# First batch of an attention block: softmax weights divided while they are turned, x formed from PSUM

## The chip, the cores and the metric

The kernel runs on one core of one Trainium2 chip. The metric is the device time of one execution in microseconds (us). TensorE (PE in the rows, PEld its weight loads), VectorE (DVE), ScalarE (ACT), GpSimd (POOL) and the queue that issues the DMAs (SP) each run their own instructions in their own order and wait for one another by semaphores.

## The reference

Attention with a decay and a causal mask over 4 batches of 8 heads (576 positions, head size 64), then a gated feed-forward net, then a soft mixture of 8 expert nets. For the change only this part matters:

```python
attn = np.exp(scores)
attn = attn / (np.sum(attn, axis=-1, keepdims=True) + 1e-09)
return np.matmul(attn, v).astype(np.float32)
...
x = np.ascontiguousarray(attn_out.transpose(0, 2, 1, 3)).reshape(B * S, H * D)
x = _moe_ref(x=x, **moe_kwargs)
```

The softmax has a row sum for each of the 576 queries of a head. The division can be made before the product with v, after it, or anywhere between.

## The kernel before

**Stages.** `merge` lays streams of steps beside each other: first `attn_unit(0)` (attention of batch 0) with three calls of `convert` (weights of the first net, read from DRAM as 1 MB pieces, turned into floats and split into two parts); then attention of batch 1 with the first net on batch 0; and so on; last the expert nets. The order in each engine's queue is then set by a scheduler that plans all instructions by its own timing, across steps. So the first heads of batch 1 and the first products of the net on batch 0 (`pm`) already stand among the last heads of batch 0.

**One head of batch 0.** `load` fetches q and k (`qk`) and the decay row (`cb`), ScalarE and GpSimd split them. `scores(h, qi)` forms one of five query tiles in PSUM (`ps_s`), a custom VectorE instruction adds the decay and takes the minimum (`np`, `mn`), ScalarE takes the exponential and leaves the row sums in a column of `sm`. `trans(h, qi)` turns each 128x128 block of `np` on TensorE into PSUM (`ps_t`), with `nc.tensor.transpose` and the identity; VectorE (tiles 2 and 4, `ONV`) or ScalarE copies the group to `pt`. Per head that is 1+2+3+4 = 10 blocks of 128x128 and 5 blocks of 64x64 (the last tile has 64 queries, on partitions 64 to 127). `pv` multiplies the turned weights with v (`vs`) into `ps_o` in two ranges of queries, 256 and 320 wide; all operands are plain float32 in batch 0. ScalarE copies the result, not yet divided, to `bt`.

**After each pair of heads** `fold` divides. `recips` takes the ten columns of sums of the pair through ScalarE (adds 1e-9) and VectorE (reciprocal), turns them on TensorE (`ps_r`), copies them (`rt`), writes them to DRAM (`rd`) and reads them back, spread over 64 partitions each, with four DMAs (`rb`). GpSimd multiplies `bt` by `rb`, ScalarE rounds the product to `xh`, and GpSimd takes the remainder `xl`. `xh` and `xl` are what the first net reads; it sums over the four pairs of heads.

Of the kernel before, what the change touches and what calls it, by code (L numbers as in the profile page):

```python
# [8 lines left out]
F32 = mybir.dt.float32  # L9
# [24 lines left out]
def attention_two_ffns(ctx: ExitStack, tc: tile.TileContext, qkT, vt, f, wf, g2, w1, w2, out):  # L34
    nc = tc.nc
    B, H, D, _, S = qkT.shape
# [4 lines left out]
    P = 128  # L41
# [21 lines left out]
    ident = const.tile([P, P], F32, name="ident")  # L63
# [18 lines left out]
    xs = {}  # L82
# [57 lines left out]
    def rest(out, src, hi, eng=None):  # L140

        (eng or nc.gpsimd).tensor_tensor(out=out, in0=src, in1=hi.bitcast(F32), op=ALU.subtract)  # L142
# [42 lines left out]
    for i in range(2):  # L185
        nc.vector.memset(sms[i], 1.0)

    pts, vss = {}, {}

    def spaces(b):  # L190
# [13 lines left out]
    def attn_unit(b):  # L204
# [3 lines left out]
        def load_pair(hp):  # L208
            if hp == 0:
                xs[b] = [(xin0, xin1)[b % 2].tile([P, KD, S], F32R, tag=t, name=t) for t in ("xh", "xl")]  # L210
                if b < 2:
                    spaces(b)
            vs = vss[hp % 2]
            vr = vs if first else vp.tile([P, 5, P], F32, tag="vr", name="vr")
            src = vt[b, :, hp * P:(hp + 1) * P]
            nc.sync.dma_start(out=vr[:, 0:4, :], in_=src[0:512].rearrange("(j p) d -> p j d", p=P))
            nc.sync.dma_start(out=vr[64:128, 4, :], in_=src[512:576])
            if not first:
                v4 = vr.rearrange("p j (h d) -> p j h d", h=2)
                nc.scalar.copy(out=vs[:, 0:4, :, 0, :], in_=v4[:, 0:4])  # L220
                for h in range(2):
                    rest(vs[:, 0:4, h, 1, :], v4[:, 0:4, h], vs[:, 0:4, h, 0, :])
                nc.scalar.copy(out=vs[64:128, 4, :, 0, :], in_=v4[64:128, 4])
                rest(vs[64:128, 4, :, 1, :], v4[64:128, 4], vs[64:128, 4, :, 0, :])
            pairs[hp] = vs, btp.tile([P, S], F32, tag="bt", name="bt", bufs=2)

        def load(h):
            qk = raw.tile([P, 2, S], F32, tag="qk", name="qk")
# [25 lines left out]
                load_pair(h // 2)  # L254

        def scores(h, qi):
            a, kh, kl, cb, mn, nps = heads[h]
            sm, col = sms[h // 2 % 2], (h % 2 * 4 + qi if qi < 4 else 8 + h % 2)
            last = qi == 4
            qs, r0 = (448, 64) if last else (qi * P, 0)  # L260
            L = min((qi + 1) * P, S)
            pt = npp.tile([P, L], F32, tag=f"np{qi}", name="np")
            nps[qi] = pt
            chunks = ((0, 288, 288), (288, 288, 288)) if last else ((0, max(L, 256), L),)
            prev = 3.0e38
            for n, (c0, w, use) in enumerate(chunks):
                ps = (ps_m if first else ps_s).tile([P, 512], F32, tag="m" if first else "s", name="ps_s")
                nc.tensor.matmul(out=ps[:, 0:w], lhsT=a[:, qs:qs + P], rhs=kh[:, c0:c0 + w], start=True, stop=False)  # L268
                if c0 + use == L:
                    m0 = qs - c0  # L270
                    nc.tensor.matmul(out=ps[:, m0:m0 + P], lhsT=identb, rhs=maskb, start=False, stop=False)
                nc.tensor.matmul(out=ps[:, 0:w], lhsT=a[:, qs:qs + P], rhs=kl[:, c0:c0 + w], start=False, stop=True)  # L272
                m = mn[r0:P, qi + n:qi + n + 1]
                nc.vector.tensor_tensor_reduce(  # L274
                    out=pt[r0:P, c0:c0 + use], in0=ps[r0:P, 0:use], in1=cb[r0:P, c0:c0 + use], scale=-SCALE,
                    scalar=prev, op0=ALU.add, op1=ALU.min, accum_out=m)
                prev = m
            nc.scalar.activation(
                out=pt[r0:P, 0:L], in_=pt[r0:P, 0:L], func=AF.Exp, scale=-1.0, bias=prev,
                accum_out=sm[r0:P, col:col + 1])  # L280
# [18 lines left out]
            return rb  # L299

        def trans(h, qi):
            pt = heads[h][-1].pop(qi)
            alt = first and qi % 3 == 2
            ps = (ps_s if alt else ps_t).tile([P, 512], F32, tag="s" if alt else "t", name="ps_t")
            n, w, r0 = (qi + 1, P, 0) if qi < 4 else (5, 64, 64)
            pv = ps[:, 0:n * w].rearrange("p (j q) -> p j q", j=n)
            for j in range(n):
                k0 = min(j * P, 448)
                nc.tensor.transpose(pv[:, j, :], pt[r0:P, k0:k0 + P], ident[r0:P, r0:P])  # L309
            c = qi * P if qi < 2 else (qi - 2) * P  # L310
            if first:
                copy = nc.vector.tensor_copy if qi in ONV else nc.scalar.copy
                copy(out=pts[qi // 2 > 0][h % 2][:, 0:n, c:c + w], in_=pv)
                return
            hi, lo = pts[qi // 2 > 0]

            nc.scalar.copy(out=hi[:, 0:n, c:c + w], in_=pv)
            nc.vector.tensor_tensor(
                out=lo[:, 0:n, c:c + w], in0=pv, in1=hi[:, 0:n, c:c + w].bitcast(F32), op=ALU.subtract)

        def pv(h, rng):
            vs, bt = pairs[h // 2]
            e = h % 2
            w, t0 = ((WA, 0), (WB, 256))[rng]
            po = ps_o.tile([P, 512], F32, tag="o", name="ps_o")
            order = [0, 1] if rng == 0 else [0, 3, 4, 1, 2]
            rows, other = slice(64 * e, 64 * e + 64), slice(64 - 64 * e, 128 - 64 * e)
            b_ap = bt[rows, t0:t0 + w]
            if first:
                for i, j in enumerate(order):  # L330
                    c0, r0 = max(0, j * P - t0), (64 if j == 4 else 0)
                    nc.tensor.matmul(
                        out=po[:, c0:w], lhsT=vs[r0:P, j, :], rhs=pts[rng][e][r0:P, j, c0:w],
                        start=(i == 0), stop=(i == len(order) - 1))
                nc.scalar.copy(out=b_ap, in_=po[rows, 0:w])
                return
            ops = [(j, part) for j in order for part in range(2)]
            for i, (j, part) in enumerate(ops):
                c0 = 64 if rng and j >= 3 else 0
                nc.tensor.matmul(  # L340
                    out=po[:, c0:w], lhsT=vs[:, j, e].rearrange("p a d -> p (a d)"), rhs=pts[rng][part][:, j, c0:w],
                    start=(i == 0), stop=(i == len(ops) - 1))
            nc.scalar.copy(out=b_ap, in_=po[other, 0:w])
            nc.vector.tensor_tensor(out=b_ap, in0=po[rows, 0:w], in1=b_ap, op=ALU.add)
# [26 lines left out]
        for h in range(H):  # L371
            steps += [(c, lambda fn=fn, h=h: fn(h)) for c, fn in
                      ((0.3, load), (1.5, head_a), (2.0, front_b), (2.0, back_b))]
            if h % 2 == 1:
                steps.append((0.3, lambda hp=h // 2: fold(hp)))
        return steps

# [377 lines left out]
```

## Time and profile before

| what | us |
|---|---|
| median of 3 runs | 2269.47 |
| lowest and highest | 2268.91, 2271.68 |
| span of the profiled execution (first to last instruction) | 2267.1 |
| TensorE busy in it | 2224.7 (98%) |
| VectorE, ScalarE, GpSimd busy | 1689.3, 852.1, 887.4 |

The profiled execution's own time is known by its span alone; the median of the runs lies 2.4 us above that span, which is what lies around the first and the last instruction. How to read it: TensorE's 98% is a share of the whole, made up of stages. In the first slices of the page the busy shares of TensorE are 7 to 9 tenths, and VectorE, ScalarE, GpSimd and the DMA engines are all at 5 to 9 tenths there; after about 300 us TensorE stands at 9 in all slices. Batch 0's attention, the only part that the change touches, lies between about 10 and 110 us.

### The profile page before, as it was taken

The numbers are of one execution on the slowest core, as the hardware profiler recorded it, in microseconds if no ns is written. First come the engines' busy times: TensorE is split into PE (matmuls) and PEld (weight loads), VectorE is DVE, ScalarE is ACT, GpSimd is POOL, SyncE is SP. The second block draws the span as 40 slices with busy tenths as digits, with TensorE's granted clock in tenths as the row PEclk, the third lists the DMA queues.
The fourth block names the chain that finished last, engine by engine and source line by source line (L and its number), as shares of the span: only waits on it lengthen the run. The fifth ranks groups of instructions, "written<-read, shape, count | busy, mean of one in ns | idle before, by whom it ended". The sixth has DMA issues, their size and how long they took to land.

```text
span 2267.1 us, 36323 instructions
## 1 busy us (share of the span) xinstructions
PE 2224.7 (98%) x13881; PEld 2020.8 (89%) x13881; DVE 1689.3 (75%) x3385; ACT 852.1 (38%) x1952; POOL 887.4 (39%) x684
## 2 busy tenths in 40 slices
PE   7898999999999999999999999999999999999999
PEld 5698899999999888898988989889989899898897
DVE  6778854544535799887888878877788787887876
ACT  7866754454322434332322323223232232322321
POOL 6869863342423444332323323333233232332320
PEclk9999999999999999999999999999999999999999
DMA  9766664454644232111111111161111111111101
GB/s 249 204 204 217 217 228 159 164 170 146 236 161 154 89 119 94 59 56 38 47 47 38 56 38 47 49 224 56 38 47 47 38 56 38 47 47 38 56 29 52
DMA packets 105102, 232.50 MB, mean 103 GB/s; under 512 B 10672, under 2 KB 60128, under 8 KB 92896
## 3 DMA queue, kind: packets, MB, share of 16 engines
q1 hardware_dynamic: 104928, 230.18, 31.5%
q8 instruction: 109, 1.79, 0.3%
q14 instruction: 65, 0.53, 0.1%
HBM read 193.27 MB, written 36.87 MB: 102 GB/s over the span
## 4 chain that ended last, share of the span: by engine, by line
PE 85%; DMA 6%; DVE 5%; POOL 1%; ACT 1%; issue 1%; SPq 1%; POOLq 0%; DVEq 0%; ACTq 0%
PE py L150 39%; PE pa L601 30%; PE pm L150 10%; DMA st<-wf 3%; PE ps_o L340 1%; PE ps_t L309 1%; PE ps_s L272 1%; DMA xst<-xd 1%; PE ps_s L268 1%; DMA rb<-rd 1%; DVE al L616 1%; DVE np L274 0%; DMA rd<-rt 0%; DVE y L111 0%; DMA lgd<-ls 0%
## 5 line engine op out<-in xcount | busy, mean ns | idle before, releaser
L601 PE MATMUL pa<-xf,w1h 128*128 128x288 f32 x3584 | 748.8, 295 | 0.2 <-DVE u L610 0.2
L601 PEld LDWEIGHTS pa<-xf,w1h 128*128 128x128 f32 x3584 | 597.7, 188 | 37.8 <-DVE u L610 0.7
L653 DVE SCALAR_TENSOR_TENSOR acc<-py,lg,acc 128x512 f32<-128x512 f32 x531 | 395.2, 744 | 247.5 <-PE py L150 247.3
L601 PE MATMUL pa<-xf,w1l 128*128 128x288 f32 x1792 | 527.6, 295 | 0.0
L142 POOL TENSOR_TENSOR w2l<-w,w2h 128x1024 fp32r<-128x1024 f32 x64 | 154.6, 2416 | 820.5 <-ACT w2h L577 820.5
L150 PE MATMUL py<-w2h,ah 128*128 128x512 f32 x1152 | 454.2, 394 | 3.3 <-DVE acc L646 2.8
L150 PE MATMUL py<-w2l,ah 128*128 128x512 f32 x1152 | 454.1, 394 | 0.0
L150 PE MATMUL py<-w2h,al 128*128 128x512 f32 x1152 | 453.2, 393 | 0.0
L616 DVE SCALAR_TENSOR_TENSOR al<-c,ah 128x288 fp32r<-128x288 f32 x512 | 431.5, 870 | 5.4 <-ACT ah L615 4.7
L615 ACT ACTIVATE ah<-c 128x288 fp32r<-128x288 f32 x512 | 208.0, 443 | 566.4 <-PE py L150 319.5
L601 PEld LDWEIGHTS pa<-xf,w1l 128*128 128x128 f32 x1792 | 337.0, 188 | 10.6
L150 PE MATMUL pm<-xh,w 128*128 128x288 f32 x1536 | 326.3, 298 | 3.3 <-DVE xa L431 1.6
L150 PEld LDWEIGHTS py<-w2h,al 128*128 128x128 f32 x1152 | 216.3, 188 | 50.0
L150 PEld LDWEIGHTS pm<-xh,w 128*128 128x128 f32 x1536 | 252.0, 188 | 6.2 <-DVE xa L431 2.1
L150 PEld LDWEIGHTS py<-w2h,ah 128*128 128x128 f32 x1152 | 216.3, 188 | 32.6 <-DVE acc L646 3.2
L150 PEld LDWEIGHTS py<-w2l,ah 128*128 128x128 f32 x1152 | 216.3, 188 | 26.1
L150 PE MATMUL pm<-xl,w 128*128 128x288 f32 x768 | 226.2, 295 | 0.5 <-POOL xl L142 0.5
L621 ACT COPY m<-pa 128x288 f32<-128x288 f32 x128 | 50.3, 393 | 437.0 <-PE pa L601 434.8
L142 POOL TENSOR_TENSOR w1l<-w,w1h 128x256 fp32r<-128x256 f32 x192 | 162.3, 873 | 125.1 <-ACT w1h L573 125.1
L150 PE MATMUL py<-ah,w 128*128 128x288 f32 x768 | 174.6, 299 | 4.8 <-DVE th L413 2.5
L142 POOL TENSOR_TENSOR al<-th,ah 128x288 fp32r<-128x288 f32 x96 | 83.6, 871 | 203.0 <-ACT ah L415 200.7
L142 POOL TENSOR_TENSOR w1l<-sm,w1h 128x1024 fp32r<-128x1024 f32 x64 | 153.7, 2401 | 2.5 <-ACT w1h L573 2.5
(145 smaller groups left out, 3109.4 us busy)
## 6 DMA issues: line engine op xcount, KB each, us to landing
w<-w SPq DMA_DIRECT2D x128, 512.0 KB, 3.5
w<-wsplit SPq DMA_DIRECT2D x54, 1024.0 KB, 5.5
qk<-qkT SPq DMA_DIRECT2D x64, 288.0 KB, 6.2
st<-wf SPq DMA_DIRECT2D x18, 1024.0 KB, 8.7
wsplit<-w SPq DMA_DIRECT2D x18, 1024.0 KB, 4.7
cb<-cumd SPq DMA_DIRECT2D x31, 288.0 KB, 4.0
xo<-h SPq DMA_DIRECT2D x28, 288.0 KB, 2.2
xf<-xo SPq DMA_DIRECT2D x14, 576.0 KB, 10.1
```

The costliest lines, as they stand in the source:

```text
L142: (eng or nc.gpsimd).tensor_tensor(out=out, in0=src, in1=hi.bitcast(F32), op=ALU.subtract)
L150: nc.tensor.matmul(out=ps, lhsT=a, rhs=b, start=(i == 0), stop=(i == n - 1))
L268: nc.tensor.matmul(out=ps[:, 0:w], lhsT=a[:, qs:qs + P], rhs=kh[:, c0:c0 + w], start=True, stop=False)
L272: nc.tensor.matmul(out=ps[:, 0:w], lhsT=a[:, qs:qs + P], rhs=kl[:, c0:c0 + w], start=False, stop=True)
L309: nc.tensor.transpose(pv[:, j, :], pt[r0:P, k0:k0 + P], ident[r0:P, r0:P])
L340: nc.tensor.matmul(out=po[:, c0:w], lhsT=vs[:, j, e].rearrange("p a d -> p (a d)"), rhs=pts[rng][part][:, j, c0:w], start=(i == 0), stop=( ...
L601: nc.tensor.matmul(out=ps, lhsT=w[:, MW[m - 1], k], rhs=x[:, m - 1, hl, k], start=(n == 0), stop=(n == len(ops) - 1))
L615: nc.scalar.activation(out=ah[:, f, tk], in_=src, func=AF.Relu)
L616: nc.vector.scalar_tensor_tensor(out=al[:, f, tk], in0=src, scalar=0.0, in1=ah[:, f, tk].bitcast(F32), op0=ALU.max, op1=ALU.subtract)
L621: nc.scalar.copy(out=m1, in_=p1)
L653: nc.vector.scalar_tensor_tensor(out=a, in0=py, scalar=lg[:, t, e:e + 1], in1=a, op0=ALU.mult, op1=ALU.add)
```

## The change

For batch 0 only, the division moves ahead of the product with v. The row sums go to a tile of their own for each head (`sm0`, named `sn0` and `sn1`). At the first and third query tile of a head VectorE adds 1e-9 to two or three columns of sums and takes their reciprocals (`rq`). For each query tile VectorE then multiplies the identity by the column of reciprocals, which gives a diagonal matrix (`dg`, 128x128 or 64x64), and the turn becomes an ordinary matmul with `np` as the stationary operand and `dg` as the moving one, where `nc.tensor.transpose` had the identity. After `pv` ScalarE rounds PSUM straight to `xh` and VectorE takes the remainder straight from PSUM to `xl`. `fold` and `recips` are no longer called for batch 0; `bt` isn't allocated there. The other batches are as before.

```diff
+    sm0 = [small.tile([P, 5], F32, name=f"sn{i}") for i in range(2)]
+    for i in range(2):
+        nc.vector.memset(sm0[i], 1.0)
...
-            pairs[hp] = vs, btp.tile([P, S], F32, tag="bt", name="bt", bufs=2)
+            pairs[hp] = vs, None if first else btp.tile([P, S], F32, tag="bt", name="bt", bufs=2)
...
-            sm, col = sms[h // 2 % 2], (h % 2 * 4 + qi if qi < 4 else 8 + h % 2)
+            sm, col = (sm0[h % 2], qi) if first else (sms[h // 2 % 2], h % 2 * 4 + qi if qi < 4 else 8 + h % 2)
...
+            turn = ident[r0:P, r0:P]
+            if first:
+                if qi in (0, 2):
+                    g0, g1 = (0, 2) if qi == 0 else (2, 5)
+                    rc = small.tile([P, 5], F32, tag="rq", name="rq", bufs=2)
+                    nc.vector.tensor_scalar_add(out=rc[:, g0:g1], in0=sm0[h % 2][:, g0:g1], scalar1=1e-9)
+                    nc.vector.reciprocal(out=rc[:, g0:g1], in_=rc[:, g0:g1])
+                    heads[h] += (rc,)
+                rc = heads[h][-1]
+                dg = small.tile([P, P], F32, tag="dg", name="dg", bufs=3)
+                nc.vector.tensor_scalar_mul(out=dg[r0:P, 0:w], in0=turn, scalar1=rc[r0:P, qi:qi + 1])
+                turn = dg[r0:P, 0:w]
             for j in range(n):
                 k0 = min(j * P, 448)
-                nc.tensor.transpose(pv[:, j, :], pt[r0:P, k0:k0 + P], ident[r0:P, r0:P])
+                if first:
+                    nc.tensor.matmul(out=pv[:, j, :], lhsT=pt[r0:P, k0:k0 + P], rhs=turn, start=True, stop=True)
+                else:
+                    nc.tensor.transpose(pv[:, j, :], pt[r0:P, k0:k0 + P], turn)
...
-                nc.scalar.copy(out=b_ap, in_=po[rows, 0:w])
+                xh, xl = (t[rows, h // 2, t0:t0 + w] for t in xs[b])
+                nc.scalar.copy(out=xh, in_=po[rows, 0:w])
+                rest(xl, po[rows, 0:w], xh, nc.vector)
                 return
+            b_ap = bt[rows, t0:t0 + w]
...
-            if h % 2 == 1:
+            if h % 2 == 1 and not first:
                 steps.append((0.3, lambda hp=h // 2: fold(hp)))
```

The scheduler lays the queues out anew. On TensorE, where the first head of batch 0 is turned and multiplied, the kernel before has these rows in succession (`ps_s` is a score tile of the second head, `vs` is v):

```order
L309 MATMUL ps_t<-ident,np 128x128 x4
L309 MATMUL ps_t<-ident,np 128x64 x5
L272 MATMUL ps_s<-kl,qkh 128x256 x2
L272 MATMUL ps_s<-kl,qkh 128x384
L268 MATMUL ps_s<-qkh 128x512
L271 LDWEIGHTS identb
L271 MATMUL ps_s<-maskb,identb 128x128
L272 MATMUL ps_s<-kl,qkh 128x512
L332 MATMUL ps_o<-pt,vs 128x320
L332 MATMUL ps_o<-pt,vs 128x192
L332 MATMUL ps_o<-pt,vs 128x64
L332 MATMUL ps_o<-pt,vs 128x320 x2
```

On TensorE, in the changed kernel, from the first turn of the first head:

```order
L326 MATMUL ps_t<-dg,np 128x128 x3
L276 MATMUL ps_s<-kl,qkh 128x256 x2
L276 MATMUL ps_s<-kl,qkh 128x384
L326 MATMUL ps_t<-dg,np 128x128 x7
L272 MATMUL ps_s<-qkh 128x512
L275 LDWEIGHTS identb
L275 MATMUL ps_s<-maskb,identb 128x128
L276 MATMUL ps_s<-kl,qkh 128x512
L350 MATMUL ps_o<-pt,vs 128x256
L350 MATMUL ps_o<-pt,vs 128x128
L326 MATMUL ps_t<-dg,np 128x64 x5
L272 MATMUL ps_s<-qkh 128x288
```

The turns now read `dg`, and the first of them stands behind three score tiles of the second head; before, six turns and the first `ps_o` of the first head stood ahead of those.

On VectorE, in the kernel before, between the last score tiles of the first head and the first of the second (`ISA` is the custom instruction on a score tile, `y`, `g` and `st` belong to `convert`, `pt` is the copy of turned weights):

```order
L274 ISA np,mn<-ps_s,cb 64x288
L274 ISA mn 64x1
L116 TENSOR_SCALAR y<-g 128x1024
L274 ISA np,mn<-ps_s,cb,mn 64x288
L274 ISA mn 64x1
L117 SCALAR_TENSOR_TENSOR st<-st,y 128x1024
L313 COPY pt<-ps_t 128x3x128
L313 COPY pt<-ps_t 128x5x64
L274 ISA np,mn<-ps_s,cb 128x128
```

On VectorE, in the changed kernel, at the same place (`sn` holds the sums, `rq` the reciprocals):

```order
L316 TENSOR_SCALAR rq<-sn_197 128x2
L278 ISA np,mn<-ps_s,cb 64x288
L278 ISA mn 64x1
L116 TENSOR_SCALAR y<-g 128x1024
L317 RECIPROCAL rq<-rq 128x2
L278 ISA np,mn<-ps_s,cb,mn 64x288
L278 ISA mn 64x1
L117 SCALAR_TENSOR_TENSOR st<-st,y 128x1024
L321 TENSOR_SCALAR dg<-ident,rq 128x128 x2
L316 TENSOR_SCALAR rq<-sn_197 128x3
L317 RECIPROCAL rq<-rq 128x3
L321 TENSOR_SCALAR dg<-ident,rq 128x128 x2
```

Nine more instructions of this head (four on `rq`, five on `dg`, the fifth right behind the last row) stand ahead of the second head's score tiles, the first two `dg` stand behind a whole convert step on `st`, and the two copies `pt` have moved behind those score tiles.

On SP, in the kernel before, around the fold of the first pair of heads:

```order
L292 DMA rd_0_177<-rt 10x128
L231 DMA qk<-qkT 64x1152 x2
L243 DMA cb<-cumd 128x576
L297 DMA rb<-rd_0_177 64x512
L298 DMA rb<-rd_0_177 64x64
L297 DMA rb<-rd_0_177 64x512
L298 DMA rb<-rd_0_177 64x64
L126 DMA wsplit_113<-w 128x2048
L103 DMA st<-wf 128x4096
```

On SP, in the changed kernel, around the same second write of converted weights:

```order
L247 DMA cb<-cumd 128x576
L235 DMA qk<-qkT 64x1152
L221 DMA vs<-vt 64x128
L126 DMA wsplit_113<-w 128x2048
L220 DMA vs<-vt 128x4x128
L235 DMA qk<-qkT 64x1152
L103 DMA st<-wf 128x4096
```

The write `rd` and the four reads `rb` are gone from the queue, four times in all, and the weights' DMAs have moved up past loads of later heads.

## Rows read from the trace of the kernel before

**Rows 1.** Busy time by stretch, from:to in us; in brackets instructions
```profile
core 0: us, PE busy (x) PEld busy (x) DVE busy (x) ACT busy (x) POOL busy (x), PEclk, DMA share, GB/s
20.00:110.00 90.00, 78.59 (x450) 59.78 (x448) 70.51 (x180) 73.42 (x181) 73.35 (x54) 0.94 0.80 228
110.00:150.00 40.00, 40.00 (x294) 38.35 (x294) 27.10 (x60) 29.48 (x73) 29.36 (x25) 0.97 0.57 178
150.00:300.00 150.00, 139.78 (x987) 127.63 (x986) 124.26 (x274) 100.75 (x233) 126.89 (x100) 0.98 0.69 223
```

**Rows 2.** The same view, three stretches of 10 us inside batch 0
```profile
40.00:50.00 10.00, 7.17 (x34) 5.58 (x34) 7.31 (x17) 5.89 (x15) 5.90 (x4) 0.71 0.95 237
50.00:60.00 10.00, 9.47 (x60) 7.40 (x58) 8.95 (x26) 9.11 (x25) 7.88 (x6) 0.95 0.84 246
70.00:80.00 10.00, 9.52 (x55) 7.33 (x55) 5.90 (x19) 8.64 (x19) 9.29 (x8) 0.92 0.81 215
```

**Rows 3.** Chain that ended last, its TensorE pieces: start us, us, what
```profile
20.96 0.89 PE ps_t L309 x9
...
23.50 2.50 PE ps_o L332 x10
...
26.66 0.67 PE ps_t L309 x6
...
78.28 0.65 PE ps_o L332 x4
```

**Rows 4.** Timeline of weight loads: the two of one 64-row product of L332
```profile
24.30 0.29 PEld L332 LDWEIGHTS ps_o<-pt,vs 64*128 64x128 f32 x2 [0.23 <-issue]
```

**Rows 5.** VectorE by line and form, first 125 us: busy us, mean ns | idle before
```profile
L274 DVE CUSTOM_DVE_ANT_0 np<-ps_s,cb 128x128 f32<-128x128 f32 x12 | 3.5, 289 | 4.6 <-PE ps_s L272 4.1 <-DMA cb<-cumd 0.4
...
L286 DVE RECIPROCAL rc<-rc 128x10 f32<-128x10 f32 x5 | 1.1, 215 | 0.1
...
L344 DVE TENSOR_TENSOR bt<-ps_o,bt 64x256 f32<-64x256 f32 x2 | 0.8, 417 | 0.0
...
L344 DVE TENSOR_TENSOR bt<-ps_o,bt 64x320 f32<-64x320 f32 x1 | 0.5, 480 | 0.0
...
L66 DVE CAST identb<-ident 128x128 bf16<-128x128 f32 x1 | 0.2, 219 | 0.0
...
L79 DVE CAST gw<-gs 128x32 fp32r<-128x32 f32 x1 | 0.2, 184 | 0.8 <-DMA gs<-g 0.8
L72 DVE MEMSET ones<- 128x128 f32 x1 | 0.2, 165 | 0.8 <-PEq L748 0.8
...
L186 DVE MEMSET sm<- 128x10 f32 x2 | 0.1, 67 | 0.0
```

**Rows 6.** GpSimd and ScalarE by line and form, first 125 us: the fold
```profile
L142 POOL TENSOR_TENSOR xl<-bt,xh 128x576 fp32r<-128x576 f32 x4 | 6.3, 1578 | 0.0
...
L350 POOL TENSOR_TENSOR bt<-bt,rb 128x576 f32<-128x576 f32 x4 | 5.7, 1414 | 4.0 <-DMA rb<-rd 4.0
...
L351 ACT CAST xh<-bt 128x576 fp32r<-128x576 f32 x4 | 2.7, 672 | 0.0
```

**Rows 7.** Timeline, last pair: DMA write, last product on TensorE, last remainder
```profile
97.67 0.47 SPq L292 DMA_DIRECT2D rd<-rt  x1
...
98.94 2.66 PE L332 MATMUL ps_o<-pt,vs 128*128 128x320 f32 x10
...
110.26 1.42 POOL L142 TENSOR_TENSOR xl<-bt,xh 128x576 fp32r<-128x576 f32 x1
```

**Rows 8.** Timeline around 42 us, VectorE and TensorE: [idle before <- releaser]
```profile
41.76 1.00 DVE L111 TENSOR_SCALAR y<-st 128x1024 uint16<-128x1024 uint16 x1 [2.37 <-DMA st<-wf]
...
43.52 0.36 PE L268 MATMUL ps_s<-qkh 128*128 128x256 f32 x1 [2.83 <-DVE mn L274]
```

**Rows 9.** Waits of TensorE from 20 to 110 us: us, times, longest
```profile
PE ps_s L268 <- DVE mn L274: 6.3, 5, 2.8
PE ps_s L272 <- POOL kl L142: 1.8, 1, 1.8
```

More of the change, by code (lines that the diff above doesn't have):

```diff
@@ L256, in scores @@
         def scores(h, qi):
-            a, kh, kl, cb, mn, nps = heads[h]
-            sm, col = sms[h // 2 % 2], (h % 2 * 4 + qi if qi < 4 else 8 + h % 2)
+            a, kh, kl, cb, mn, nps = heads[h][:6]
+            sm, col = (sm0[h % 2], qi) if first else (sms[h // 2 % 2], h % 2 * 4 + qi if qi < 4 else 8 + h % 2)
             last = qi == 4
@@ L301, in trans @@
         def trans(h, qi):
-            pt = heads[h][-1].pop(qi)
+            pt = heads[h][5].pop(qi)
             alt = first and qi % 3 == 2
@@ L327, in pv @@
             rows, other = slice(64 * e, 64 * e + 64), slice(64 - 64 * e, 128 - 64 * e)
-            b_ap = bt[rows, t0:t0 + w]
             if first:
```

## The prediction

> **What bounds the kernel now.** I read the busy time by stretch first, since the 98% of the page hides the stage that the change touches. From 20 to 110 us, where batch 0's attention runs, TensorE is busy 78.6 of 90 us, VectorE 70.5, ScalarE 73.4, GpSimd 73.4, and the DMA engines 80% [rows 1]: five resources, each between 78% and 87%, none full. From 110 to 150 TensorE is busy without a gap, and from 150 to 300 it is busy 139.8 of 150 us. So a delay of the first stage is handed on: what comes after is TensorE's work in full, with some 10 us of idle up to 300 us that could take a little back. The question is how long the first stage becomes.
>
> In that stage TensorE has 11.4 us of idle (90 less 78.6). The largest part, 6.3 us, is waiting for VectorE to free a score buffer, and 1.8 us for GpSimd's split of k [rows 9]. One of those waits shows how it comes about: VectorE sat 2.37 us on a convert step whose weights had not landed, the score tiles stood behind it in its queue, and TensorE idled 2.83 us [rows 8]. Just after this the granted clock was 0.71 on average over 10 us [rows 2], that is, TensorE ran part of them at 1.2 GHz; over the stage it was 0.94 [rows 1]. The best that single stretches show is TensorE busy 9.52 of 10 us and VectorE 8.95 of 10 [rows 2]; I use these as the fullest the two get in this mixture of work.
>
> **TensorE: the turns become float32 products.** The chain of waits gives paces without the drain at the end. Six turns of 128x128 took 0.67 us, 0.112 each; nine turns, four of them 128x128 and five 64x64, took 0.89 us, which leaves (0.89 - 4 x 0.112) / 5 = 0.088 for a small one [rows 3]. The products of weights and v are float32 too and are ordinary matmuls, and each of their instructions appears as two passes: two instructions (256 and 128 columns) have x4 and took 0.65 us for 768 columns, 0.85 ns a column, so 0.108 us for a pass of 128 columns [rows 3]. A turn by a diagonal is such a product with 128 columns: two passes, 0.216 us, where a transpose takes 0.112. Batch 0 has 8 heads x 10 = 80 of them: 80 x 0.104 = +8.3 us.
>
> For the small turns (64 rows, 64 columns, 8 x 5 = 40) the row is the one product of the kind in each `pv`. Five products with ten passes took 2.50 us; eight passes with 2304 columns at 0.85 ns are 1.95, which leaves 0.55 for the two small passes, 0.27 each [rows 3], with the change of rows in and out in it. The other end is the pace of their weight loads: two took 0.29 us, with a single one at about 0.18, so they start 0.11 apart [rows 4]. Five turns in succession change rows once, so I take 0.13, near the load's end: per head 10 x 0.13 - 5 x 0.088 = 0.86, times 8 = +6.9 us (from 5.3 at 0.11 to 18.1 at 0.27). The four turns `ps_r` go, each a pass of 128 columns: 4 x 0.108 = -0.4 us. TensorE's sum is +14.8 us, with ends +13 and +26.
>
> The page "FP8 and Floating Point Precision" of the Trainium skill (section TensorE Precision Notes) gives true float32 four passes, and "TensorE: Matmul & The Clock Gate" (section Terms) calls its transpose mode four times faster for float32. The trace agrees with the first (two records at twice the time per column) but not with the second: a turn of 128 columns at 0.112 us is half a product's 0.216, not a quarter. By the pages the large turns would add 80 x 0.162 = 13 us where the rows give 8.3.
>
> **VectorE: diagonals, reciprocals, remainders.** None of these operations is in the trace of batch 0, so each has bounds [rows 5]. A diagonal of 128x128 (32 of them) lies between a memset of that size, 0.165, and the custom instruction on a 128x128 score tile, 0.289; I take 0.219, the copy of the same identity. 32 x 0.219 = 7.0. The eight small ones: 0.184, a 128x32 copy, 1.5 in sum (0.067 below). Sixteen additions on two or three columns: 0.184 by the same row, 2.9 (0.067 by a memset of ten columns). Sixteen reciprocals: 0.215 as the ten-column one, 3.4 (0.067 again below). Sixteen remainders `xl` from PSUM: eight at 0.417 and eight at 0.480, as the same form at L344, 7.2. Gone are four reciprocals and four copies `rt`, which I count like them: 8 x 0.215 = -1.7. The sum is +20 us, with ends +13 and +23.
>
> **The rest.** GpSimd loses four multiplications and four remainders, 5.7 + 6.3 = 12 us; ScalarE loses four roundings, 2.7 us [rows 6], and its 16 copies to `bt` become 16 roundings of the same size. SP loses 20 DMAs with their waits. I put these at nothing: neither engine is the one that TensorE mostly waits for, and at most the 1.8 us of rows 9 goes with them. If their cover were gone the other way there is nothing to pay, since they only lose work. The fold's latency also goes: the last pair's `rd` was issued at 97.67 and its last remainder ended at 110.26 + 1.42 = 111.7 us [rows 7]; with the change `x` is there about a copy and a remainder after the product. But TensorE has other work by then, and is busy throughout from 110 on, so that an earlier `x` finds no idle TensorE.
>
> **A new wait.** Each turn now waits for its diagonal, and this for reciprocals, and these for the last exponential of a group of two or three tiles. Queued behind the waiting diagonals on VectorE are the score tiles of the next head, the convert steps and the copies `pt`; TensorE waits for all of them. The new order answers by putting three score tiles of the second head ahead of the first turn, which holds more score buffers at a time.
>
> **The sum.** In the stage VectorE has 70.5 + 20 = 90.5 us to do in what were 90; at 0.895 busy that needs 101.1 us, +11.1. TensorE has 78.6 + 14.8 = 93.4; at 0.952 it needs 98.1 us, +8.1. The larger counts, since each waits for the other in turn: +11 us. Nothing later gives it back. On the profiled span, 2267.1 + 11 = 2278.1, and with the 2.4 us between span and median, **2280.5 us**. With both engines at the low ends (83.7 / 0.895 and 91.6 / 0.952) the stage grows by 4 to 6 us: 2275; with the high ends (93.5 / 0.895 and 104.6 / 0.952) by 14 to 20, of which I take 17, since 0.27 for every small pass counts the change of rows each time: 2287.
>
> **Rivals.**
> (1) *The new chain stalls the queues.* The idle that TensorE has stays on top of its sum: 93.4 + 11.4 = 104.8, +14.8; and in half of the eight heads the diagonals of the third group come late by one wait of the kind in rows 9 (6.3 / 5 = 1.26 us), +5. That gives +20, **2290 us**. For it: the 2.83 us of rows 8, where one VectorE instruction that waited held everything. Against it: the scheduler has put other work between.
> (2) *The clock makes up for part.* The granted clock over the stage is 0.94, and TensorE's low clock follows its pauses in the one case of rows 8 and 2. If fuller queues keep it at 2.4 GHz, TensorE's sum falls by 0.06 x 78.6 = 4.7 to 88.7, or 93.2 us at 0.952, +3; VectorE must then be near its low end (+3.5). That gives **2273 us**, within 0.2%. The Trainium skill, "TensorE: Matmul & The Clock Gate" (section Part 4: PE-mode transpose), speaks for it: transposes don't count as TensorE being busy in the way that matmuls do. By that rule the change turns 120 uncounted instructions into counted ones. The trace neither shows nor denies it: the fall in rows 2 has a plain pause before it.
> (3) *Faster: the fold was the pace.* If TensorE's 14.8 us fit into its 11.4 us of idle and the 4.7 us that the low clock costs, the stage stays at 90 us; then the 14 us from `rd` to the last remainder [rows 7] and GpSimd's 12 us [rows 6] let the first net run ahead, and half of the 10 us of idle from 150 to 300 [rows 1] closes: -5, **2264 us**. It decides as soon as VectorE has room for its 20 us; it has 19.5 us of idle in 90, and no stretch shows it full. That is what speaks against it.
> (4) *The change doesn't do what it says on TensorE*, that is, a product by a diagonal runs in one pass like a transpose. VectorE's sum stands, +11; this changes the reason and not the time, and has its chance inside the forecast.
>
> **How the numbers follow.** The forecast with its own range 2275 to 2287 gets 0.52, the stalled chain 0.16, the clock 0.18, the faster case 0.14. About 0.2% (4.5 us, so 2265 to 2274) is what a measurement of this kernel can tell from no change. Slower is the forecast and the stall, 0.68; same the clock, 0.18; faster 0.14. The range leaves out the faster case and the far side of the stall: 2265 to 2293.
>
> **What would show it.** Turns with two passes each and a pace near 0.22 us for 128 columns, near 0.26 for the small ones; diagonals near 0.22 us; VectorE busy some 90 us by the time the last `ps_o` of batch 0 ends, and this end some 11 us later than the 101.6 us of now [rows 7]; from there on the same distance to the end as before. The prediction is wrong if VectorE does its new work in its idle time and that end doesn't move, if the granted clock rises to 1.0 and TensorE's busy time in the stage stays below 90 us, or if the stretch from 150 to 300 closes its idle.

## The result, and the profile after

The changed kernel takes 2284.9 us (median of 5 runs, 2283.21 to 2287.61), the kernel before in the same comparison 2269.33 (5 runs, 2267.80 to 2271.68): a ratio of 1.007 with a 95% interval of 1.0057 to 1.0084, or +15.6 us. The forecast was 2280.5, slower. The profiled execution, 1.5 us above that median, has a span of 2284.6 us, against 2267.1.

Busy time of the engines of the changed kernel over the span, from its page:

```profile
PE 2241.1 (98%) x13997; PEld 2038.1 (89%) x13997; DVE 1711.1 (75%) x3467; ACT 850.1 (37%) x1944; POOL 870.2 (38%) x676
```

TensorE is busy 16.4 us longer than before and VectorE 21.8. Of the span, 17.5 us longer, TensorE was idle 2284.6 - 2241.1 = 43.5 us, where it was 42.4. So at the end TensorE's idle is what it was, and its added work is there in full. It is tempting to stop here and blame the second passes; the experiments say otherwise.

The same stretches as [rows 1, 2], now of the changed kernel:

```profile
core 0: us, PE busy (x) PEld busy (x) DVE busy (x) ACT busy (x) POOL busy (x), PEclk, DMA share, GB/s
20.00:110.00 90.00, 75.61 (x430) 60.63 (x429) 81.11 (x199) 54.93 (x127) 47.75 (x37) 0.92 0.64 194
110.00:150.00 40.00, 39.31 (x266) 33.92 (x265) 24.44 (x82) 29.54 (x76) 20.52 (x21) 1.00 0.42 120
150.00:300.00 150.00, 140.40 (x1008) 129.87 (x1006) 124.94 (x276) 104.97 (x246) 123.84 (x96) 0.98 0.67 220
40.00:50.00 10.00, 7.19 (x40) 5.57 (x40) 9.68 (x27) 7.48 (x17) 5.38 (x4) 0.76 0.37 93
50.00:60.00 10.00, 9.16 (x55) 7.54 (x54) 7.27 (x15) 3.13 (x6) 4.25 (x4) 0.90 0.75 247
70.00:80.00 10.00, 7.89 (x51) 6.39 (x51) 9.81 (x29) 6.45 (x18) 5.04 (x4) 1.00 0.72 263
```

From 20 to 110 us VectorE is now the fullest engine, 81.1 of 90 us where it had 70.5; in two of the short stretches it has no room left (9.68 and 9.81 of 10). ScalarE fell from 73.4 to 54.9 and GpSimd from 73.4 to 47.8: they have done less by then, in part because they have less to do. TensorE's idle rose from 11.4 to 14.4 us although it has more to do.

TensorE's waits from 20 to 125 us in the changed kernel (us, times, longest), to be set beside [rows 9]:

```profile
PE ps_t L326 <- DVE dg L321: 4.5, 6, 1.3
PE ps_s L272 <- DVE mn L278: 4.1, 7, 1.1
PE ps_t L326 <- DVE pt L332: 3.9, 2, 2.7
PE ps_o L350 <- DVE xl L142: 1.6, 1, 1.6
```

All of them end on VectorE, on four kinds of its work, and GpSimd's split of k is gone from the list. The new operations on VectorE up to 125 us (busy us, mean ns | idle before):

```profile
L321 DVE TENSOR_SCALAR dg<-ident,rq 128x128 f32<-128x128 f32 x32 | 20.3, 658 | 0.3
...
L316 DVE TENSOR_SCALAR rq<-sn 128x3 f32<-128x3 f32 x8 | 4.2, 521 | 0.9 <-ACT np L282 0.9
...
L321 DVE TENSOR_SCALAR dg<-ident,rq 64x64 f32<-64x64 f32 x8 | 3.9, 484 | 2.8 <-PE ps_t L326 2.6
...
L142 DVE TENSOR_TENSOR xl<-ps_o,xh 64x320 fp32r<-64x320 f32 x7 | 3.4, 484 | 0.2
...
L316 DVE TENSOR_SCALAR rq<-sn 128x2 f32<-128x2 f32 x8 | 2.0, 247 | 0.0
...
L317 DVE RECIPROCAL rq<-rq 128x3 f32<-128x3 f32 x8 | 1.4, 170 | 0.1
...
L317 DVE RECIPROCAL rq<-rq 128x2 f32<-128x2 f32 x8 | 1.3, 157 | 0.1
```

A diagonal of 128x128 takes 0.658 us on average, not 0.219, and all 40 take 24.2 us where the prediction had 8.5. The mean hides two kinds. Of the 40, 23 take 0.25 to 0.29 us, and 17 take 0.44 to 1.50. The timeline shows what parts them. First VectorE, then GpSimd, of the changed kernel near 57 us:

```profile
57.15 2.60 DVE L321 TENSOR_SCALAR dg<-ident,rq 128x128 f32<-128x128 f32 x2
```

```profile
57.16 1.41 POOL L142 TENSOR_TENSOR kl<-qk,qkh 128x576 fp32r<-128x576 f32 x1
58.52 2.26 POOL L122 TENSOR_TENSOR st<-st,g 128x512 f32<-128x512 f32 x2
```

And VectorE near 48.8 us, where GpSimd ran nothing from 47.5 to 50.5:

```profile
48.41 0.17 DVE L316 TENSOR_SCALAR rq<-sn 128x3 f32<-128x3 f32 x1
48.61 0.18 DVE L317 RECIPROCAL rq<-rq 128x3 f32<-128x3 f32 x1
48.83 0.48 DVE L321 TENSOR_SCALAR dg<-ident,rq 128x128 f32<-128x128 f32 x2
```

Alone, two diagonals take 0.48 us. Beside GpSimd the same two take 2.60: by the single records the first ends at 58.65, 0.08 us after the GpSimd instruction `kl` (57.16 + 1.41 = 58.57), and the second 0.08 us after the next one. All 17 long ones end like this, 0.05 to 0.09 us after a GpSimd instruction that was in progress when they began (in one case began 6 ns later). Five that began 0.07 to 0.17 us ahead of a GpSimd instruction, and ran on into it, took 0.25 to 0.28. The additions `rq` show the wait too: on three columns 0.17 alone and 0.52 on average. The reciprocals don't: five of them began beside a GpSimd instruction and took 0.15 to 0.17 us, as the others did. VectorE stands still in these waits while it counts as busy.

On TensorE the turns show as 160 and 80 records, two for each product, as predicted. Their pace, from the chain of waits:

```profile
113.10 2.15 PE ps_t L326 x18
```

Eight passes of the last full tile at 0.108 leave (2.15 - 0.87) / 10 = 0.13 us for a small one, which is the value taken.

### The profile page after: what moved, and what is told of

It reads as the page before. It is cut to its first block, busy times and chain, and to the rows that moved or that the text cites. A ratio compares the mean times of both kernels' runs of the same rounds, so it can differ in the third digit from the quotient of the medians.

```text
span 2284.6 us, 36612 instructions
## 1 busy us (share of the span) xinstructions
PE 2241.1 (98%) x13997; PEld 2038.1 (89%) x13997; DVE 1711.1 (75%) x3467; ACT 850.1 (37%) x1944; POOL 870.2 (38%) x676
## 4 chain that ended last, share of the span: by engine, by line
PE 83%; DVE 7%; DMA 4%; issue 2%; POOL 2%; ACT 1%; SPq 0%; DVEq 0%; POOLq 0%; ACTq 0%
PE py L150 39%; PE pa L622 29%; PE pm L150 10%; DMA st<-wf 1%; PE ps_o L361 1%; PE ps_t L328 1%; DVE np L278 1%; DMA xst<-xd 1%; PE ps_s L276 1%; PE ps_s L272 1%; DVE al L637 1%; DMA w<-w 1%; DVE dg L321 1%; DVE g L114 1%; POOL w L142 1%
## 6 DMA issues: line engine op xcount, KB each, us to landing
st<-wf SPq DMA_DIRECT2D x18, 1024.0 KB, 10.3
```

## The experiments

All times are medians of 5 runs or more, each beside the kernel before in the same comparison: 2268.1 us for the three new kernels of the square of four and for ScalarE's diagonals, 2269.2 for the passes in the kernel before, ScalarE without additions, divided rows and PSUM, 2269.3 for GpSimd, tensor products and the last two. Differences in brackets are to that; the changed kernel has +15.6. Two theories compete at first: V, that VectorE's new instructions cost the time, and P, that TensorE's second passes do.

**Diagonals and passes apart.** Between them these three kernels and the changed one are the four combinations of "VectorE makes reciprocals and diagonals" and "turns are products". All four form x straight from PSUM and have no fold. The three new ones leave the division of batch 0 out; they are there for their time alone.

Products by the plain identity, no `rq`, no `dg`:

```diff
-            if first:
-                ...
-                turn = dg[r0:P, 0:w]
```

> The changed kernel without reciprocals and diagonals: the turns of batch 0 are float32 matmuls by the identity, x comes straight from PSUM and is not divided (the division of batch 0 is left out). It keeps TensorE's two passes (13.6 us more than transposes by the paces of the changed kernel's trace) and takes VectorE's 48 small instructions of batch 0 away. Theory V (VectorE's reciprocals and diagonals, which mostly wait for a GpSimd instruction to end, set the stage): 2266 to 2274 us, near the kernel before. Theory P (the doubled passes on TensorE set the stage): 2280 to 2285 us, near the changed kernel. Both in part: between, 2275 to 2279.

Transposes, while VectorE makes `rq` and `dg` that nobody reads:

```diff
-                turn = dg[r0:P, 0:w]
...
-                if first:
-                    nc.tensor.matmul(out=pv[:, j, :], lhsT=pt[r0:P, k0:k0 + P], rhs=turn, start=True, stop=True)
-                else:
-                    nc.tensor.transpose(pv[:, j, :], pt[r0:P, k0:k0 + P], turn)
+                nc.tensor.transpose(pv[:, j, :], pt[r0:P, k0:k0 + P], turn)
```

> The changed kernel with the turns as transposes by the identity again; VectorE still makes all reciprocals and diagonals, but nobody reads the diagonals (the division of batch 0 is left out). Theory V: 2279 to 2285 us, since VectorE's work stays. Theory P: 2264 to 2272 us, since the passes are gone. A third theory, that the wait of TensorE for the diagonals (the chain from the sums to the turn) is what costs, and neither engine's work: 2264 to 2272 here and 2264 to 2272 without diagonals too.

Both edits, so that only the fold is gone and x comes from PSUM:

> Second half of the change alone: transposes by the identity, no reciprocals, no diagonals, no fold; x of batch 0 goes straight from PSUM to xh (ScalarE) and xl (VectorE), not divided (the division of batch 0 is left out). All theories: the fold's removal itself costs nothing; VectorE gains 7.2 us of work and GpSimd loses 12. V and P: 2262 to 2270 us. If the straight x itself (VectorE's remainders, 7.2 us) were a good part of the loss: 2273 us or more.

| | transposes | products |
|---|---|---|
| no `rq`, no `dg` | 2268.3 (+0.2; 12 runs; ratio 0.999 to 1.001) | 2261.3 (-6.8; 0.9956 to 0.9981) |
| VectorE makes `rq`, `dg` | 2290.7 (+22.6; 1.0081 to 1.0114) | 2284.9 (+15.6; 1.0057 to 1.0084) |

By the differences to the kernel before, VectorE's 72 new instructions on `rq` and `dg` (not the 48 of the expectation) add 22.4 us down either column, and the second passes take away 7.0 along either row. From the kernel before to the changed one that makes +0.2 for the fold, -7.0 for the passes and +22.4 for VectorE's work. Theory V holds in kind and P falls, here. V's ranges missed in both kernels that set it against P, 2261.3 for 2266 to 2274 and 2290.7 for 2279 to 2285, since it had no gain from passes. TensorE's part is seen in the busy time by stretch, first of the kernel with products and without diagonals:

```profile
20.00:110.00 90.00, 86.44 (x547) 70.36 (x546) 68.84 (x184) 69.68 (x168) 62.22 (x46) 0.98 0.69 210
```

Then of the two with transposes, without diagonals and with unread ones:

```profile
20.00:110.00 90.00, 72.49 (x399) 53.42 (x399) 64.48 (x165) 63.32 (x154) 53.94 (x42) 0.94 0.71 208
```

```profile
20.00:110.00 90.00, 72.33 (x353) 53.90 (x353) 82.39 (x211) 58.12 (x138) 47.94 (x37) 0.81 0.65 197
```

Down the column of products, from VectorE at 68.8 us to 81.1, TensorE's idle grows from 3.6 of 90 us to 14.4 and the granted clock falls from 0.98 to 0.92. Down the column of transposes the idle stays, 17.5 us and 17.7, but the clock falls from 0.94 to 0.81 and TensorE has 353 instructions in it where it had 399. With the unread diagonals it waits 13.6 us on score buffers, where it was 3.0 without them:

```profile
PE ps_s L272 <- DVE mn L278: 13.6, 10, 2.5
```

So what VectorE's work costs comes out on TensorE as idle time in one column and mostly as a lower clock in the other. Over the first 300 us the granted clock is 0.99 and 0.97 in the column of products, 0.98 and 0.92 in that of transposes: at most some 6 and some 18 us of TensorE's time, an estimate from these shares. With parts so unlike, that both columns come to 22.4 may be chance. The idle by itself isn't the loss either: with 17.5 us of it in the stage the kernel with neither is level with the kernel before, which has 11.4. The run with unread diagonals also shows that TensorE doesn't have to wait for a diagonal for this: nothing reads them.

**Passes in the kernel before.** The same products by the identity, with the fold as it was:

```diff
-                nc.tensor.transpose(pv[:, j, :], pt[r0:P, k0:k0 + P], ident[r0:P, r0:P])
+                if first:
+                    nc.tensor.matmul(
+                        out=pv[:, j, :], lhsT=pt[r0:P, k0:k0 + P], rhs=ident[r0:P, r0:P], start=True, stop=True)
+                else:
+                    nc.tensor.transpose(pv[:, j, :], pt[r0:P, k0:k0 + P], ident[r0:P, r0:P])
```

> The kernel before with one edit: the turns of batch 0 are float32 matmuls by the identity (two passes) and not transposes; the fold stays. Without diagonals, matmul turns were 7.0 us faster than transposes (2261.3 against 2268.3), against the price by passes (+13.6). If that is the granted clock, as the skill's page says that transposes don't count as work of TensorE (the stretches at 1.2 GHz before 300 us are 3.4 + 3.4 us there against four of 3.4 us), or another effect of the turns themselves, it is here too: 2259 to 2265 us, with less time at 1.2 GHz than the kernel before has (five stretches, 20.4 us). If it was the plan of the scheduler that happened to be better: 2268 to 2275 us here. If the passes cost as predicted: 2278 to 2283 us.

2280.9 us (+11.6), ratio 1.0043 (1.0029 to 1.0057): here the passes cost something near their length, where they gained 7.0 without the fold. The rows of this kernel:

```profile
20.00:110.00 90.00, 85.87 (x515) 69.94 (x513) 58.36 (x154) 65.94 (x155) 66.28 (x49) 0.94 0.72 216
110.00:150.00 40.00, 39.32 (x290) 35.98 (x289) 26.80 (x78) 34.36 (x90) 27.95 (x26) 1.00 0.69 213
150.00:300.00 150.00, 140.82 (x971) 129.08 (x969) 125.17 (x276) 103.57 (x237) 125.89 (x97) 0.94 0.67 210
```

Two things differ from the run without a fold: the clock is lower (0.94 against 0.98 from 20 to 110 us, and 0.94 in the stretch where before had 0.98), and VectorE is busy 10 us less from 20 to 110 us (58.4 against 68.8). About half of that is work that this kernel doesn't have (1681.0 us busy over the whole kernel, against 1686.0); the rest comes later. Every edit makes the scheduler lay out all queues anew, and which of this is the fold and which the order isn't told apart.

**Diagonals on other engines.** On ScalarE:

```diff
-                nc.vector.tensor_scalar_mul(out=dg[r0:P, 0:w], in0=turn, scalar1=rc[r0:P, qi:qi + 1])
+                nc.scalar.mul(out=dg[r0:P, 0:w], in_=turn, mul=rc[r0:P, qi:qi + 1])
```

> The changed kernel with the 40 diagonals made by ScalarE (identity times the column of reciprocals) in place of VectorE; the reciprocals stay on VectorE. ScalarE had 55 of 90 us busy in the stage and takes some 40 x 0.3 = 12 us more. Theory V: the stage shortens by most of the 24 us that the diagonals took on VectorE, 2270 to 2277 us. Theory P: no change, 2282 to 2287 us.

2278.4 us (+10.3), 1.0048 (1.0035 to 1.006): 5.3 us of the 15.6 come back, with intervals that just overlap, and theory V had asked for 2277 or less. ScalarE's diagonals don't vary (0.38 to 0.41 us); the additions left on VectorE wait longer than ever (0.854 against 0.17 alone):

```profile
L321 ACT ACTIVATE dg<-ident,rq 128x128 f32<-128x128 f32 x32 | 12.4, 397 | 3.3 <-DVE rq L317 1.7 <-PE ps_t L326 1.2 <-ACT dg L321 0.4
...
L316 DVE TENSOR_SCALAR rq<-sn 128x3 f32<-128x3 f32 x8 | 6.8, 854 | 2.1 <-ACT np L282 2.1
```

On ScalarE, and the additions taken away as well (the reciprocal reads the sums):

```diff
-                    nc.vector.tensor_scalar_add(out=rc[:, g0:g1], in0=sm0[h % 2][:, g0:g1], scalar1=1e-9)
-                    nc.vector.reciprocal(out=rc[:, g0:g1], in_=rc[:, g0:g1])
+                    nc.vector.reciprocal(out=rc[:, g0:g1], in_=sm0[h % 2][:, g0:g1])
```

> dg_act (diagonals on ScalarE, 2278.4 us) without the 16 additions of 1e-9, which took VectorE 0.854 and 0.500 us on average there, 10.8 us in all: the reciprocal reads the sums directly. (A sum is at least 1 here, since the row's largest weight is 1, and 1e-9 is below float32's step at 1.) VectorE then has no instruction of the new ones that waits for GpSimd but the reciprocals, which took 0.16 to 0.17. Theory V with the lock: 10 us less in VectorE's queue, 2266 to 2272 us, level with the kernel before. If the additions were hidden: 2276 to 2280 us.

2275.5 us (+6.3; 12 runs), 1.0024 (1.0014 to 1.0033): 9.3 us have come back, 3.5 us short of V's range. It is the fastest of the kernels that divide ahead of the product with v, and still slower than before.

On GpSimd (`nc.gpsimd.tensor_scalar_mul` in the same place):

> The changed kernel with the diagonals made by GpSimd instead of VectorE. VectorE loses 24 us of work, GpSimd, which lost 12 us by the change, gets 40 instructions of some 0.4 to 0.8 us, 16 to 32 us. If VectorE's work is what costs: 2274 to 2282, like the run with the diagonals on ScalarE (2278). If GpSimd's work holds up VectorE as much as it relieves it: 2283 to 2290.

2283.2 us (+13.9), 1.0064 (1.0052 to 1.0076): little comes back. The diagonals cost GpSimd 29.4 us, and VectorE's additions pay for its being busy (0.778 and 0.633 us):

```profile
L321 POOL TENSOR_SCALAR dg<-ident,rq 128x128 f32<-128x128 f32 x32 | 23.4, 741 | 4.1 <-PE ps_t L326 3.6 <-DMA st<-wf 0.2
L316 DVE TENSOR_SCALAR rq<-sn 128x3 f32<-128x3 f32 x8 | 6.2, 778 | 2.9 <-ACT np L282 2.1 <-POOL dg L321 0.8
L321 POOL TENSOR_SCALAR dg<-ident,rq 64x64 f32<-64x64 f32 x8 | 6.0, 746 | 0.8
L316 DVE TENSOR_SCALAR rq<-sn 128x2 f32<-128x2 f32 x8 | 5.1, 633 | 0.9 <-POOL dg L321 0.5 <-ACT np L282 0.3
```

**No diagonals.** ScalarE divides the rows of `np` in place, ahead of a transpose:

```diff
+                nc.scalar.mul(out=pt[r0:P, 0:L], in_=pt[r0:P, 0:L], mul=rc[r0:P, qi:qi + 1])
```

> Another way to divide before the product, as a candidate: ScalarE scales the rows of np in place by the column of reciprocals (no diagonals, no additions), and the turns are transposes by the identity again; x straight from PSUM. ScalarE gets 40 instructions of 128 to 576 columns, by its exponentials of the same shapes 0.40 to 0.77 us each, 24 us, in a stage where it had 55 of 90 us busy in the changed kernel and 73 in the kernel before. VectorE has 2.6 us of reciprocals and 7.2 of remainders. Theory V: 2268 to 2275 us (as the straight x alone, 2268.3, and something for ScalarE's load). If ScalarE becomes the bound: 2280 us or more.

2287.3 us (+18.1), 1.0071 (1.0055 to 1.0087). VectorE and the passes are relieved (58.6 and 70.9 us busy from 20 to 110), and ScalarE is the fullest engine in their place with 76.4 us; the time is no better. So with VectorE relieved of all diagonals the division ahead of the product still costs as much; which engine or wait holds the stage up here isn't shown.

**What the diagonals wait for.** Three edits of the diagonal alone. First its source moved to PSUM:

```diff
+    pso = ps_o.tile([P, 512], F32, tag="o", name="ps_o")
+    idp = pso[:, 384:512]
+    nc.vector.tensor_copy(out=idp, in_=ident)
...
-            po = ps_o.tile([P, 512], F32, tag="o", name="ps_o")
+            po = pso
...
-                nc.vector.tensor_scalar_mul(out=dg[r0:P, 0:w], in0=turn, scalar1=rc[r0:P, qi:qi + 1])
+                nc.vector.tensor_scalar_mul(out=dg[r0:P, 0:w], in0=idp[r0:P, r0:P], scalar1=rc[r0:P, qi:qi + 1])
```

> The changed kernel with one edit: VectorE multiplies a copy of the identity that lies in PSUM (spare columns of the ps_o bank) by the column of reciprocals, so that the diagonal has no operand read from SBUF but the column; same engine, same count, same waits. Theory V with the lock (a diagonal read from SBUF waits for the GpSimd instruction in progress, 0.95 to 1.50 us, where one that doesn't takes 0.28): all 40 take 0.26 to 0.32 us, VectorE has 12 us less, 2272 to 2277 us. If the duration came from something else (the matmul that frees the buffer, the column operand): durations as in the changed kernel, 0.66 on average, and 2283 to 2287 us.

The forms, and a place where GpSimd was busy throughout (VectorE, then GpSimd):

```profile
L325 DVE TENSOR_SCALAR dg<-ps_o,rq 128x128 f32<-128x128 f32 x32 | 9.6, 339 | 0.2
L325 DVE TENSOR_SCALAR dg<-ps_o,rq 64x64 f32<-64x64 f32 x8 | 2.3, 291 | 0.3
```

```profile
64.43 0.41 DVE L142 TENSOR_TENSOR xl<-ps_o,xh 64x256 fp32r<-64x256 f32 x1
64.77 0.91 DVE L325 TENSOR_SCALAR dg<-ps_o,rq 128x128 f32<-128x128 f32 x3
```

```profile
63.92 1.74 POOL L142 TENSOR_TENSOR w<-st,w 128x512 fp32r<-128x512 f32 x1
```

None of the 40 waits: they take 0.29 to 0.35 us, though 18 of them began with a GpSimd instruction in progress; the three above take 0.91 together while one runs until 65.66. The additions, whose input still lies in SBUF, go on waiting here (up to 1.38 us). That confirms the mechanism for the diagonal. The time, though, is 2311.7 us (+42.5), 1.0192 (1.017 to 1.0214), worse than any other, and TensorE waits for the diagonals (20 to 135 us):

```profile
PE ps_t L330 <- DVE dg L325: 21.2, 15, 3.0
```

where it was 4.5 us in the changed kernel (20 to 125 us). The order on VectorE shows why: 15 of the 16 groups of diagonals stand directly behind a remainder `xl`, as above, where in the changed kernel two of 22 do. So a head's diagonals come only after the product `ps_o` ahead of them has been computed, rounded and read. The identity lies in the bank of `ps_o`, and that this sharing is what ties them is the likely reason, not a tested one. As a measure of what the waiting costs this run fails.

Then an edit that keeps the order of every queue, instruction by instruction: the diagonal as the product of two tensors.

```diff
-                nc.vector.tensor_scalar_mul(out=dg[r0:P, 0:w], in0=turn, scalar1=rc[r0:P, qi:qi + 1])
+                nc.vector.tensor_mul(out=dg[r0:P, 0:w], in0=turn, in1=rc[r0:P, qi:qi + 1].to_broadcast([P - r0, w]))
```

> The changed kernel with each diagonal made by a tensor_tensor product of the identity and the column of reciprocals spread along the row, in place of a tensor_scalar product. Every instruction of every engine keeps its place in its queue. Theory L (the price of the diagonals on VectorE is that a tensor_scalar instruction waits until GpSimd's instruction ends, and a tensor_tensor one doesn't): the diagonals take 0.25 to 0.40 us each, none above 0.6, some 12 us in sum where it was 24; the kernel takes 2274 to 2280 us. Theory Q (what costs is the place of the diagonals in VectorE's queue and what they wait for; their own length is hidden): they get shorter, and the time stays at 2283 to 2288. Theory S (the wait falls on any VectorE instruction beside GpSimd): they still average 0.55 us or more, and the time stays.

2283.9 us (+14.6), 1.0064 (1.0051 to 1.0078), the same as the changed kernel:

```profile
L321 DVE TENSOR_TENSOR dg<-ident,rq 128x128 f32<-128x128 f32 x32 | 23.6, 766 | 0.3
...
L321 DVE TENSOR_TENSOR dg<-ident,rq 64x64 f32<-64x64 f32 x8 | 2.6, 330 | 3.6 <-PE ps_t L326 3.4
```

Theory L falls: with both inputs in SBUF this form waits as well, 18 of the 40, and by the records the large ones end 0.15 us after GpSimd. S holds for both forms of the diagonal, but not for any VectorE instruction: the reciprocals, whose input lies in SBUF too, never wait. For the diagonals it decides where the identity lies. How much the waiting of the diagonals costs in an unchanged order thus stays unmeasured.

Last, the additions alone away, and both edits together:

> The changed kernel without the 16 additions of 1e-9: the reciprocal reads the sums directly; the diagonals stay on VectorE as tensor_scalar. The additions took 6.2 us of VectorE. If VectorE's busy time sets the stage: 2278 to 2282. If only the diagonals matter: 2283 to 2287.

> Both edits: diagonals as tensor_tensor, no additions. Theory L with VectorE setting the stage: 2269 to 2276, near the kernel before. Theory Q or S: 2279 to 2286.

2283.1 us (+13.8), 1.0061 (1.0049 to 1.0073), and 2281.4 (+12.1), 1.0054 (1.0041 to 1.0067). The additions' 6.2 us on VectorE are worth 1.8 us, and 2.5 beside the tensor products; the intervals overlap with those of the kernels that have them, so neither is settled. With the diagonals on ScalarE their absence gave 4.0 (from +10.3 to +6.3), where they took 10.8 us.

No run that does the whole work beats the kernel before.

## Why the prediction was right, and where it was not

The time, 2284.9 us, is 4.4 above the forecast, inside its own range of 2275 to 2287. That VectorE's new work is what costs is what the four combinations show, in kind. That VectorE's fullness sets the length of the stage they don't show: over the other kernels the time doesn't follow VectorE's busy time from 20 to 110 us (58.6 us with divided rows at +18.1, 69.5 with GpSimd's diagonals at +13.9, 70.5 in the kernel before). And VectorE's sum came out near by two errors that cancel, which is luck.

- **TensorE's sum: right.** Two records for each turn, 0.13 us for a small pass, and +14.8 us forecast where TensorE is busy 16.4 longer. Rival 4 falls. But the sum is no cost in itself: without diagonals and fold the same passes gained 7.0 us, and with the fold they cost 11.6.
- **VectorE's diagonals: the mis-sized term.** I took 0.219 from a copy made in the quiet first microseconds of the kernel and bounded it by 0.289 from an instruction that reads PSUM. Alone a diagonal is 0.25 to 0.29, but in place 0.61 on average over all 40: +15.7 us over the forecast of 8.5. The additions gave 6.2 for 2.9; reciprocals 2.7 for 3.4; remainders 7.2 as forecast. The new work is 24.2 + 6.2 + 2.7 + 7.2 = 40 us, or 38 without what the fold had, far beyond the upper end of +23.
- **VectorE's other work taken as unchanged: wrong, and it hid the first error.** VectorE's whole busy time grew by 21.8 us, close to the +20 of the sum, because other VectorE instructions became shorter, by some 16 us in all. The convert steps of the kernel before and then of the changed one, up to 125 us:

```profile
L117 DVE SCALAR_TENSOR_TENSOR st<-st,y 128x1024 f32<-128x1024 uint32 x6 | 11.1, 1853 | 0.2
L114 DVE SCALAR_TENSOR_TENSOR g<-st,g 128x1024 uint16<-128x1024 uint16 x6 | 10.7, 1777 | 0.4 <-ACT g L113 0.4
```

```profile
L114 DVE SCALAR_TENSOR_TENSOR g<-st,g 128x1024 uint16<-128x1024 uint16 x6 | 8.5, 1410 | 0.7 <-ACT g L113 0.7
...
L117 DVE SCALAR_TENSOR_TENSOR st<-st,y 128x1024 f32<-128x1024 uint32 x6 | 7.8, 1297 | 0.1
```

  These two give 5.5 us back in the stage; the rest isn't followed here. That GpSimd's lost work is what shortened them isn't shown: in the kernel before with products, which keeps the fold, the two take 17.9 us, near the 16.3 of the changed kernel and not the 21.8 of before. The means of before, far above the 1.23 us that the shortest of either form took, were there to be read: they should have told me that a form on VectorE can take much longer in place than alone.
- **The sum of the stage: right in kind.** VectorE's fullness of 0.895 is what it reached (81.1 of 90). TensorE reached 0.84, not 0.952, and its waits end on VectorE. The 100th product of the first net started at 132.3 us before and at 150.9 now, +18.6, more than the +11 of the sum.
- **"Nothing later gives it back": a little wrong.** The first products of the expert nets started 21.1 us later, the thousandth and the five thousandth 17.4.
- **The end of the last `ps_o` is no good mark.** It moved from 101.60 [rows 7] to 126.72 + 2.73 = 129.45, by 28 us and not by 11, while the first net's products behind it moved by 19: the new order lets it run later among other work.
- **Rival 1** (a stalled chain): it has a part. Waits on `dg` are 4.5 us, six of up to 1.3, the size that it named. But unread diagonals cost as much, so the chain isn't the main thing. Its other part, that TensorE's idle stays on top of its sum, is how the totals look (42.4 and 43.5 us), but by the four combinations it isn't the passes that cost.
- **Rival 2** (the clock): not borne out. The granted clock from 20 to 110 us went from 0.94 to 0.92. The rule of the Trainium skill, "TensorE: Matmul & The Clock Gate" (section Part 4: PE-mode transpose), would have the clock rise with products. It did along both rows of the four combinations (0.94 to 0.98 without diagonals, 0.81 to 0.92 with them), and it did not in the kernel before with products (0.94 in both, and down from 0.98 to 0.94 from 150 to 300 us). So the runs don't agree on this rule. Nor does the clock follow TensorE's idle alone: 0.94 and 0.81 came with 17.5 and 17.7 us of it.
- **Rival 3** (the fold was the pace): not borne out. With the fold away and its remainders on VectorE the time stays at a ratio of 1.000 (0.999 to 1.001). Products without VectorE's diagonals do come out faster, at 2261.3 us beside the 2264 of this rival, which made it depend on VectorE's room; that this is its reason isn't shown.

What stays open is the size. Each of these kernels has one layout of its queues, and only the tensor products keep that of the changed kernel, with diagonals that wait as before; the passes cost 11.6 us or gain 7.0 depending on what else is in the queues. Nor do 22.4 us come back when another engine makes the diagonals, but 5.3 at ScalarE's (9.3 without additions) and little at GpSimd's. So I can say that VectorE's new work makes the difference, and not how much of it is its length, its waiting for GpSimd, or its place in the order.

## What to carry to other kernels

Before you price an instruction on VectorE by one that ran in a quiet part, look how busy GpSimd is where it will stand, and whether a form that is there already has a mean far above its shortest: take the price from there. When an edit moves work, look at the lengths of the other instructions of its stage too: here they changed by some 16 us and hid a term that was mis-sized by as much. An edit that is to measure one wait must not bring a new one, as the identity in the bank of `ps_o` seems to have done. And where a scheduler lays out the queues anew, compare edits in a square of four combinations, since a single one can't tell the work from the new order; a square still has one order in each corner.

## What the runs showed of the hardware

A product on VectorE whose inputs all lie in SBUF waited for a GpSimd instruction that was in progress when it began, and at 128x128 ended 0.08 us (tensor by column scalar) or 0.15 us (tensor by tensor) after it: 0.22 to 0.29 us became up to 1.52. An addition on two or three columns waited as well, and ended 0.02 to 0.03 us after. A product that began at least 0.07 us ahead of the GpSimd instruction didn't wait (0.22 to 0.28), nor did a reciprocal from SBUF (0.15 to 0.18), nor the product with its tensor in PSUM (0.29 to 0.35). The Trainium skill, "SBUF — State Buffer" (section Who interferes with whom), says that VectorE and GpSimd share a pair of ports, held for a whole instruction, for which scalar products in a fast mode and instructions with two inputs in SBUF compete; the numbers of the two products agree with it. I had not drawn on it in the prediction: 40 diagonals at their price alone are 11 us, and the rest of the 24.2, some 13, is 17 waits of 0.8 us on average, a little over half of a GpSimd instruction of 1.4 like `kl` above. That last step is an estimate, after the fact.
